# Dealing one store's rows unevenly over the 16 DMA engines: dV of head 15 in a decode-attention gradient kernel

## The chip, the cores and the metric

The kernel runs on one core of a Trainium2 chip. The metric is the device time of one execution, in microseconds (us). Each figure below is the median of several executions, with lowest and highest in brackets. The kernel before took 402.59 us (402.49 to 402.77, 3 runs) when it was handed over. Every run quoted here counts as a fast one (none lies over 1.5% above the fastest of its kernel). The profile of a run spans about 2 us less than its device time (400.6 against 402.6).

## The reference, cut to what matters

```python
def _A_ref(x, k_cache, v_cache, wq, wo):        # one query token, H=32 heads, Sk=4096, Dh=128, D=640, bf16
    q = (x @ wq).reshape(B, Sq, H, Dh).transpose(0, 2, 1, 3)
    p = softmax(einsum("bhqd,bhkd->bhqk", q, k_cache) * Dh ** -0.5)
    o = einsum("bhqk,bhkd->bhqd", p, v_cache)
    return o.transpose(0, 2, 1, 3).reshape(B, Sq, H * Dh) @ wo
# _B_ref: a dense layer 640 -> 1728 -> 640 with mish;  g = sigmoid((x * gate_w).sum(-1))
return g * a + (1 - g) * b
# reference(): this output, and its gradients by x, k_cache, v_cache, wq, wo, w1, b1, w2, gate_w
```

K and V have 32 x 4096 x 128 elements of 2 bytes, 33.6 MB each, and their gradients dK and dV are as large. So of the 164.93 MB that the kernel moves, 134 MB are these four, and some 31 MB are the weights and their gradients. One head is 1 MB (1024 KB) of K, of V, of dK and of dV.

## The kernel before

Loads of K, V and the weights are issued by the sync engine (SP), on one hardware queue. Nearly all gradients are stored by the gpsimd engine (POOL), on the software queue. Both queues run on the same 16 DMA engines. A tile of one head has 128 rows (partitions) of 8192 B. A plain DMA of it puts 8 rows on each of the 16 engines.

```python
KB, VB = 4, 4
outs = ctx.enter_context(tc.tile_pool(name="outs", bufs=5))        # dK and dV tiles on their way out

def load_k(h):                                                      # load_v is alike
    if h < H:
        kts[h] = kv_in.tile([P, J, Dh], BF16, name="Kn", tag="Kn", bufs=KB)
        nc.sync.dma_start(kts[h][:], Kv[h])

def load_wo(g):                                                     # g: a group of G = 4 heads
    if g < NG:
        wos[g] = wts.tile([P, G, D], BF16, name="wo_g", tag="wo_g", bufs=3)
        nc.sync.dma_start(wos[g][:], wo_v[g])
...
def dwo():                                 # the gradient overwrites the weight tile and is stored from it
    for i in range(G):
        nc.vector.tensor_scalar(wos[g][:, i, :], da_bc[:], fs["o4"][:, i:i + 1], None, ALU.mult)
    (nc.sync if g == NG - 1 else nc.gpsimd).dma_start(dwo_v[g], wos[g][:])
...
for h in range(H):
    hh, g = h % G, h // G
    if hh == 3:
        load_wo(g + 2)                     # waits for the dwo store that still reads this buffer ...
        if g % 2 == 0:
            load_wq(g // 2 + 1)
    load_k(h + 3)                          # ... and these stand behind it in the same queue
    load_v(h + 3)
    ...
    period(h)
...
dwq_l = wts.tile([P, RC, GD], BF16, name="dwq_l", tag="wo_g", bufs=3)
...
nc.sync.dma_start(dwq_v[:, :, CL:], dwq_l[:])                       # the last store of the kernel
```

A new `wo_g` tile can be loaded only when the store of an older `dwo` out of the same buffer has landed on all the engines. And the K and V loads of the next head are issued after that load by the same sequencer.

The kernel before already deals a few dV stores unevenly (heads 5, 12, 19 and 26). It cuts the rows into several DMAs; for heads 5 and 26 it first resets the cursor, the place from which the software queue starts dealing rows to engines:

```python
if half == 1:
    if h % 7 == 5 and h < H - 3:
        spread(h // 7, dVv[h], st["dV"])
    else:
        ring(h).dma_start(dVv[h], st["dV"][:])

def spread(i, dst, t):
    ...
    if i % 3 == 0:
        nc.gpsimd.inc_swdge_sem([], [], mode="reset_dge_cursor")
    for a, b in (((120, 125), (0, 120), (125, 128)), ((0, 14), (14, 119), (119, 128)), ((0, 8), (8, 128)))[i % 3]:
        nc.gpsimd.dma_start(out[a:b, :], src[a:b, :], max_dma_last_dim=J * Dh)
```

## Time and profile before

| | |
|---|---|
| device time | 402.59 us |
| bytes moved | 164.93 MB, 412 GB/s on average |
| DMA share of the stretches between 12 and 385 us | 1.01 to 1.02 |
| busiest compute engines | DVE 303.5 us, PE 296.6 us |
| last computation ends, last store issued, last store landed | 387.3, 391.9, 399.5 us |

These are lines of the page of the kernel before: busy time of each engine, the span in 40 slices of 10.0 us (digits are busy tenths), and the queues with packets, MB and share. `q1` is the queue of the loads, `q0` the software queue of the stores, `q8` fetches instructions.

```profile
span 400.6 us, 13611 instructions
PE 296.6 (74%) x5872; PEld 268.1 (67%) x5872; DVE 303.5 (76%) x791; ACT 177.1 (44%) x411; POOL 47.2 (12%) x94
DMA  8999999999999999999999999999999999999995
GB/s 288 420 415 397 421 426 417 418 423 422 425 419 424 421 422 419 419 424 422 427 415 426 422 423 419 418 428 422 421 424 423 422 421 417 423 422 416 425 378 232
DMA packets 28360, 164.93 MB, mean 412 GB/s; under 512 B 3260, under 2 KB 3964, under 8 KB 12556
q1 hardware_dynamic: 17136, 93.41, 56.5%
q0 software_dynamic: 11104, 70.64, 42.3%
q8 instruction: 46, 0.75, 0.7%
```

The DMA engines are full from start to end, and DVE and PE have a quarter of the span free.

No view names DMA engines. In the packet records, however, a packet starts 3 or 4 ns before its predecessor on the same engine ends, so the packets can be sorted into 16 streams. For the kernel before that gives:

- The 46 instruction fetches (16 KB, 0.99 us each) go round robin to eight of the 16 engines, six each to six of them ("heavy") and five each to two. I call these eight the fetching engines.
- Seven engines without fetches ("light") end by 396 us.
- One more without fetches, at position 4 counted from the reset cursor, has some 15 us of stretched packets (packets that take longer than usual for their size). The existing spreads give it less. It ends at 399.1 us.

### The profile page before, as it was taken

What the parts mean: (1) busy time and instruction counts of PE and PEld (TensorE: products, weight loads), DVE (VectorE), ACT (ScalarE), POOL (GpSimd) and SP (SyncE); (2) the same over time, 40 slices, a digit from 0 to 9 for tenths busy, and PEclk for the clock granted to TensorE, in tenths of its full rate; (3) what the DMA queues carried; (4) which work ended last, traced back from release to release, by engine and by line L of the source; (5) the groups of instructions that cost most, each with busy time, mean ns of one, the idle gap of its engine ahead of it and who ended that gap; (6) DMA issues with size and microseconds to landing.
All of it is one profiled execution on the core that took longest, in us unless ns stands there. A gap on an engine that the chain in (4) does not pass through costs nothing.

```text
span 400.6 us, 13611 instructions
## 1 busy us (share of the span) xinstructions
PE 296.6 (74%) x5872; PEld 268.1 (67%) x5872; DVE 303.5 (76%) x791; ACT 177.1 (44%) x411; POOL 47.2 (12%) x94
## 2 busy tenths in 40 slices
PE   0688898778888788778885988819887888888200
PEld 0588787668777678668875878718776777777200
DVE  2438766646799999856688799837999997899850
ACT  1355555324554455325543555605545455545000
POOL 0001101021110111211110113101110121111000
PEclk9999999959999999959998899977999999999655
DMA  8999999999999999999999999999999999999995
GB/s 288 420 415 397 421 426 417 418 423 422 425 419 424 421 422 419 419 424 422 427 415 426 422 423 419 418 428 422 421 424 423 422 421 417 423 422 416 425 378 232
DMA packets 28360, 164.93 MB, mean 412 GB/s; under 512 B 3260, under 2 KB 3964, under 8 KB 12556
## 3 DMA queue, kind: packets, MB, share of 16 engines
q1 hardware_dynamic: 17136, 93.41, 56.5%
q0 software_dynamic: 11104, 70.64, 42.3%
q8 instruction: 46, 0.75, 0.7%
q14 instruction: 14, 0.11, 0.1%
q10 hardware_dynamic: 60, 0.01, 0.0%
HBM read 82.03 MB, written 82.03 MB: 410 GB/s over the span
## 4 chain that ended last, share of the span: by engine, by line
DVE 36%; DMA 34%; PE 17%; issue 5%; ACT 4%; SPq 0%; POOL 0%; ACTq 0%; POOLq 0%
DMA Kn<-in_A_k_cache_dram 29%; DVE dK_sb L612 9%; DVE dV_sb L612 8%; PE tr L587 7%; DVE junk L385 4%; DMA out_dram<-wo_g 4%; ACT tT L589 4%; PE sA L667 3%; DVE junk L288 3%; PE sA L596 2%; PE sB L720 2%; DVE junk L537 2%; DMA vec_rows<-in_gate_w_dram 1%; DVE wo_g L374 1%; DVE dj L707 1%
## 5 line engine op out<-in xcount | busy, mean ns | idle before, releaser
L589 ACT COPY tT<-tr 128x512 f32<-128x512 f32 x256 | 142.3, 588 | 133.9 <-PE tr L587 133.1
L596 PEld LDWEIGHTS <-tT 128*128 128x128 bf16 x2048 | 79.8, 98 | 40.1 <-ACT tT L589 34.6
L587 PE MATMUL tr<-ident_f,Kn 128*128 128x128 f32 x512 | 82.0, 298 | 9.7 <-DMA Kn<-in_A_k_cache_dram 9.7
L612 DVE TENSOR_TENSOR dV_sb<-p_bf,qd 128x2048 bf16<-128x2048 bf16 x64 | 78.0, 1218 | 0.2 <-issue 0.2
L612 DVE TENSOR_TENSOR dK_sb<-ds_bf,qd 128x2048 bf16<-128x2048 bf16 x64 | 77.7, 1216 | 0.0
L587 PE MATMUL tr<-ident_f,Vn 128*128 128x128 f32 x512 | 72.5, 277 | 0.0
L587 PEld LDWEIGHTS tr<-ident_f,Kn 128*128 128x128 f32 x512 | 61.2, 152 | 11.2 <-issue 11.2
L596 PE MATMUL sA<-qd,tT 128*128 128x48 bf16 x1024 | 48.8, 187 | 23.7 <-ACT dq_all L725 12.7
L587 PEld LDWEIGHTS tr<-ident_f,Vn 128*128 128x128 f32 x512 | 55.9, 141 | 0.0
L596 PE MATMUL sB<-qd,tT 128*128 128x48 bf16 x1024 | 46.1, 183 | 0.0
L667 PEld LDWEIGHTS <-Vn 128*128 128x128 bf16 x1024 | 30.2, 95 | 10.4 <-issue 10.4
L667 PE MATMUL sA<-e_bf,Vn 128*128 128x48 bf16 x1024 | 30.7, 183 | 7.7 <-DVE zs L687 6.1
L629 POOL DMA_DIRECT2D out_dram<-dK_sb x30 | 17.3, 576 | 138.6 <-DVE rz L689 90.6
L720 PE MATMUL sB<-ds_bf,Kn 128*128 128x48 bf16 x1024 | 32.1, 185 | 1.4 <-DVE ds_bf L709 1.4
L671 DVE TENSOR_REDUCE m<-sA 128x1 f32<-128x32 f32 x32 | 6.1, 189 | 35.2 <-PE sA L596 28.5
L720 PEld LDWEIGHTS <-Kn 128*128 128x128 bf16 x1024 | 29.4, 97 | 1.6 <-issue 1.6
L642 POOL DMA_DIRECT2D out_dram<-dV_sb x26 | 14.1, 544 | 136.8 <-DVE o_all L712 50.0
L288 DVE SCALAR_TENSOR_TENSOR junk<-wo_g,da_bc 128x640 bf16<-128x640 bf16 x32 | 26.3, 821 | 2.6 <-ACT da_bc L229 1.1
L385 DVE SCALAR_TENSOR_TENSOR junk<-wq_g,dq_bc 128x1024 bf16<-128x1024 bf16 (+1 forms) x25 | 25.1, 1005 | 0.2
L707 DVE TENSOR_SCALAR_CACHE_REDUCE dj<-sB,rz 128x128 f32<-128x128 f32 x32 | 11.1, 346 | 9.2 <-PE sB L701 9.2
L691 ACT ACTIVATE p_bf<-e_bf,rz 128x64 bf16<-128x64 bf16 x32 | 11.1, 348 | 13.6 <-DVE rz L689 10.7
L698 DVE SCALAR_TENSOR_TENSOR pj<-sB,e_bf 128x32 f32<-128x32 f32 x32 | 6.1, 190 | 12.5 <-PE sB L596 12.4
(152 smaller groups left out, 275.5 us busy)
## 6 DMA issues: line engine op xcount, KB each, us to landing
Kn<-in_A_k_cache_dram SPq DMA_DIRECT2D x32, 1024.0 KB, 23.1
Vn<-in_A_v_cache_dram SPq DMA_DIRECT2D x32, 1024.0 KB, 27.5
out_dram<-dK_sb POOLq DMA_DIRECT2D x30, 1024.0 KB, 11.7
out_dram<-dV_sb POOLq DMA_DIRECT2D x26, 1024.0 KB, 11.8
wq_g<-in_A_wq_dram SPq DMA_DIRECT2D x4, 1280.0 KB, 23.7
wo_g<-in_A_wo_dram SPq DMA_DIRECT2D x8, 640.0 KB, 16.7
out_dram<-wo_g POOLq DMA_DIRECT2D x7, 640.0 KB, 12.2
out_dram<-dwq_t SPq DMA_DIRECT2D x4, 896.0 KB, 18.3
```

The costliest lines, as they stand in the source:

```text
L288: nc.vector.scalar_tensor_tensor(junk[:, 0:D], in0=wos[g][:, i, :], scalar=1.0, in1=da_bc[:], op0=ALU.mult, op1=ALU.mult, accum_out=gp["do ...
L385: nc.vector.scalar_tensor_tensor(junk[:, c0:c1], in0=wqs[w][:, rc, c0:c1], scalar=1.0, in1=dq_bc[:, w * WG * Dh + c0:w * WG * Dh + c1], op ...
L587: nc.tensor.transpose(tp[:, t, :], flat[:, k * P:(k + 1) * P], ident_f[:])
L589: nc.scalar.copy(sb[:].rearrange("p a b -> p (a b)"), tp[:].rearrange("p a b -> p (a b)"))
L596: nc.tensor.matmul(out[:, 2 * k:2 * k + W], lhsT=tb[:, t, par, :], rhs=vec[:, par, :].unsqueeze(1).to_broadcast([P, W // 2, 2]), start=(pa ...
L612: nc.vector.tensor_tensor(dst[:, a:b, :].rearrange("p j (a b) -> p j a b", b=2), col[:, a:b, :].unsqueeze(2).to_broadcast([P, n, Dh // 2, 2]),
L629: ring(h).dma_start(dKv[h], st["dK"][:])
L642: ring(h).dma_start(dVv[h], st["dV"][:])
L667: nc.tensor.matmul(O, lhsT=vts[h][:, j, :], rhs=st["e"][:, j:j + 1].to_broadcast([P, W]), start=(j == 0), stop=(j == J - 1))
L691: nc.scalar.activation(p_bf[:], e[:].unsqueeze(2).to_broadcast([P, J, 2]), ACT.Copy, scale=rz[:])
L707: nc.vector.tensor_scalar(dj[:], PT, rz[:], None, ALU.mult, ALU.add, accum_out=dd[:])
L720: nc.tensor.matmul(DQ, lhsT=kts[h][:, j, :], rhs=ds[:, j, 0:1].to_broadcast([P, W]), start=(j == 0), stop=(j == J - 1))
```

## The change

The intent is to even the load of the engines: head 15's dV gets 17 rows on each of the seven engines at positions 8 to 14 and one row on each of positions 0 to 7. The last row is cut into 16 pieces of 512 B, one for each engine. Heads 12 and 19 get the same cut as heads 5 and 26, and the cursor is reset at each of these stores.

```diff
         if half == 1:
-            if h % 7 == 5 and h < H - 3:
-                spread(h // 7, dVv[h], st["dV"])
+            if h in SPREAD:
+                spread(SPREAD[h], dVv[h], st["dV"])
             else:
                 ring(h).dma_start(dVv[h], st["dV"][:])
 
-    def spread(i, dst, t):
+    S15 = ((120, 125), (0, 120), (125, 128))
+    SPREAD = {5: S15, 12: S15, 15: ((0, 8), (8, 127), (127, 128)), 19: S15, 26: S15}
+
+    def spread(parts, dst, t):
 ...
-        if i % 3 == 0:
-            nc.gpsimd.inc_swdge_sem([], [], mode="reset_dge_cursor")
-        for a, b in (((120, 125), (0, 120), (125, 128)), ((0, 14), (14, 119), (119, 128)), ((0, 8), (8, 128)))[i % 3]:
+        nc.gpsimd.inc_swdge_sem([], [], mode="reset_dge_cursor")
+        for a, b in parts:
             nc.gpsimd.dma_start(out[a:b, :], src[a:b, :], max_dma_last_dim=J * Dh)
```

## The prediction

> **What bounds the kernel.** The page gives 164.93 MB in 400.6 us, 412 GB/s; the stretch table a DMA share of 1.01 or 1.02 in every stretch from 12 to 385 us, against 303.5 us busy on DVE and 296.6 on PE. In the timeline the last computation (the copy of fin_rows) ends at 387.3 us; 13 us of pure stores follow. So DMA bounds it, and its most loaded engines end it: dwq_l is computed by 381.2 us but issued at 391.9, when an earlier store on its semaphore has landed on all engines, and lands at 399.5.
>
> **Which engines are most loaded.** No view names DMA engines. But in the packet records a packet starts 3 or 4 ns before its predecessor on the same engine ends, so I separated the packets into 16 streams, each with the sizes that its queues require. (Positions below count from the reset cursor.)
> - The 46 instruction packets (16 KB, 0.99 us each) go round robin to eight engines, about 5.5 us each; the others get none.
> - These eight end together, at 398 to 399 us, without idle time. Seven have no fetches, run up to 16 us ahead in the loads and end by 396. One more (position 4) has no fetches, but 14 us of stretched packets; the existing spreads avoid it.
> - The Trainium skill ("DMA: Bandwidth & Descriptors", "Why a DMA increments its semaphore by 16 and not by 1") says that SWDGE uses k consecutive engines from a round-robin cursor. The trace agrees: of head 5, the 5 rows land on positions 0 to 4, the 120 on all but 4, the 3 on 4 to 6. From heads 5, 12 and 19: positions 0 to 3 are light, 4 slow, 5 and 6 fetch, 7 to 12 hold four fetching and two light, 13 to 15 two fetching and one light.
>
> **What the change does.** Positions 8 to 14 get 17 rows of head 15 instead of 8, the others one. (The last row is split into 16 pieces of 512 B.) Making heads 12 and 19 alike takes one row from positions 7 to 15. By the sets above, 8 to 14 hold at least three of the four fetching engines in 7 to 12 and one in 13 to 15: at least four of the eight that end the kernel. Four light engines (0 to 3) are relieved, who need it least.
>
> **Cost.** A row as two 4096 B packets takes 2 x 156 ns, as one of 8192 B 306 ns. A heavy fetching engine gains 17 x 0.311 - 8 x 0.306 - 0.31 = +2.5 us. It never idles and both its queues must drain, so nearly all of it reaches the end: later loads, and the landing that releases dwq_l, come up to 2.5 us later. Relieving the rest helps nothing, as the slowest engine decides. Compute instructions are unchanged; the extra POOL issues are hidden.
>
> **Prediction.** 402.6 + 2.5 = about 405.0 us, 402.7 to 406.4. Faster by over 2%: 0.01; within 2%: 0.97; slower by over 2%: 0.02.
>
> **What would show it.** dV of head 15 lands some 10 us later than before (now 12 to 17 us after issue); dwq_l issued near 394 instead of 391.9, landing near 402; bytes and DVE and PE busy time unchanged.
>
> **What would make it wrong.** If positions 8 to 14 were just the seven light engines, the slowest would lose 7 rows and the time fall by 1 to 2 us, to about 401. If the 119 rows were dealt as 8 rows to each of 15 engines, nothing would change.

## More of the kernel before

The sync queue's waits of the kernel before (engine, line, what it waited for, then us in total, times, and the longest in us). L121 is `load_k`, L136 is `load_wo`.

```profile
SPq L121 <- PE sB L720: 168.3, 20, 17.8
SPq L136 <- DMA out_dram<-wo_g: 58.0, 5, 13.3
```

The second line is the wait for the dwo store. It takes 58.0 us in five waits, and during each of them no load is issued. In the timeline of the sync engine (start, duration, line, what) it looks like this around 230 us:

```profile
224.72 0.33 SPq L121 DMA_DIRECT2D Kn<-in_A_k_cache_dram  x1
225.10 0.50 SPq L126 DMA_DIRECT2D Vn<-in_A_v_cache_dram  x1
238.00 0.33 SPq L136 DMA_DIRECT2D wo_g<-in_A_wo_dram  x1
238.42 0.43 SPq L131 DMA_DIRECT2D wq_g<-in_A_wq_dram  x1
238.94 0.69 SPq L121 DMA_DIRECT2D Kn<-in_A_k_cache_dram  x1
```

And the chain of waits of the kernel before passes through it:

```profile
223.24 14.71 DMA out_dram<-wo_g
...
238.94 31.03 DMA Kn<-in_A_k_cache_dram
```

From one load to the next there are 12.9 us, and the two slices from 220 to 240 us still have 422 and 423 GB/s, as the queue of loads already issued lasts that long.

## The result, and the profile after

The changed kernel took 407.40 us (407.14 to 407.88, 4 runs) against 402.68 us (402.49 to 403.44, 4 runs) of the kernel before on the same chip. The ratio is 1.0115, with an interval of 1.0098 to 1.0133. A ratio here is the mean time of one kernel's fast runs over that of the other's of the same rounds, so it is not quite the ratio of the medians quoted. The change costs 4.7 us, or 1.2%. That is inside the band of 2% in which kernels count as the same, and 1.0 us above the top of the predicted range.

The page of the kernel after (40 slices of 10.1 us):

```profile
span 405.5 us, 13618 instructions
PE 295.8 (73%) x5872; PEld 267.6 (66%) x5872; DVE 303.5 (75%) x791; ACT 177.1 (44%) x411; POOL 49.2 (12%) x97
DMA  7999999999999999999999999999999999999984
GB/s 293 420 416 401 421 422 420 420 420 424 420 423 423 422 422 416 422 424 422 422 418 422 424 415 350 380 423 421 422 422 422 424 422 421 420 422 419 423 345 181
DMA packets 28936, 164.93 MB, mean 407 GB/s; under 512 B 3694, under 2 KB 4414, under 8 KB 13260
```

The bytes and the work of DVE and PE are unchanged. The row of GB/s shows something that nobody had predicted: in the 25th and 26th slice (243 to 264 us) the rate falls to 350 and 380 GB/s, where it was 419 and 418. The digits of the DMA row stay at 9 there: the engines are busy but slow. The missing rate is (419 - 350 + 418 - 380) GB/s over 10.14 us, or 1.08 MB, and at 420 GB/s that is worth 2.6 us.

The changed store is issued at 197 us, and the dip comes 45 us later. What lies between is in the waits and the timeline of the sync queue after the change:

```profile
SPq L121 <- PE sB L722: 158.4, 20, 16.6
SPq L136 <- DMA out_dram<-wo_g: 70.5, 5, 23.0
```

```profile
221.61 0.33 SPq L121 DMA_DIRECT2D Kn<-in_A_k_cache_dram  x1
221.99 0.64 SPq L126 DMA_DIRECT2D Vn<-in_A_v_cache_dram  x1
245.68 0.33 SPq L136 DMA_DIRECT2D wo_g<-in_A_wo_dram  x1
246.10 3.73 SPq L131 DMA_DIRECT2D wq_g<-in_A_wq_dram  x1
249.92 2.41 SPq L121 DMA_DIRECT2D Kn<-in_A_k_cache_dram  x1
```

No load was issued for 23.7 us (221.99 to 245.68), where it had been 12.9 us (225.10 to 238.00). The `dwo` store of group 4 was issued at nearly the same time, but it landed late. From the semaphore's 16 increments, one per engine (my own reading of the trace):

```
                                  issued   first engine landed   last engine landed
dV of head 15, before             197.33   209.50                214.37
dV of head 15 (119 rows), after   197.01   214.14                222.31
dwo of group 4, before            223.24   233.10                237.95
dwo of group 4, after             223.65   235.19                245.62
```

The Trainium skill ("DMA: Bandwidth & Descriptors", "Why a DMA increments its semaphore by 16 and not by 1") says that only the full 16 means that all data has landed, and that all 16 engines post their increment on the software queue whatever the shape. The trace agrees: `load_wo` is issued at 245.68 us, 0.06 us after the sixteenth increment, although the first engine had done its part 10 us earlier.

The lines of the stores in the issues of each kernel (KB each, median us from issue to landing). Before:

```profile
out_dram<-dV_sb POOLq DMA_DIRECT2D x26, 1024.0 KB, 11.8
out_dram<-wo_g POOLq DMA_DIRECT2D x7, 640.0 KB, 12.2
```

After. The third line is the DMA of 119 rows:

```profile
out_dram<-dV_sb POOLq DMA_DIRECT2D x25, 1024.0 KB, 13.0
out_dram<-wo_g POOLq DMA_DIRECT2D x7, 640.0 KB, 13.2
out_dram<-dV_sb POOLq DMA_DIRECT2D x1, 952.0 KB, 25.3
```

The table by stage (length, busy us and instructions of PE, PEld, DVE, ACT and POOL, granted clock, DMA share, GB/s), of the stretch in which the sync queue waits and of the one after it. Before:

```profile
238.00:246.00 8.00, 6.39 (x145) 5.74 (x144) 7.59 (x21) 3.43 (x9) 1.87 (x3) 1.00 1.01 422
246.00:256.00 10.00, 8.71 (x183) 7.84 (x181) 8.20 (x21) 7.27 (x15) 2.78 (x5) 1.00 1.02 418
```

After:

```profile
238.00:246.00 8.00, 6.89 (x133) 6.33 (x130) 7.66 (x20) 4.29 (x10) 1.92 (x3) 1.00 0.99 392
246.00:256.00 10.00, 8.76 (x180) 7.89 (x177) 8.22 (x24) 6.80 (x14) 2.27 (x4) 1.00 1.00 358
```

Compute hardly differs, so it did not cause the dip. The DMA engines read as busy (1.00) at 358 GB/s. The streams tell more: the leading engines have no load left from 233 us on, and from 246 to 249 us fewer than one of the 16, on average, is moving one. Among the packets of the software queue, which then run alone on most engines, those of 4096 B are stretched: of 158 between 243 and 252 us, 67 took over 190 ns, many of them 300 to 600, where 159 is usual. Those of 8192 B took 8% longer than usual on average. The packets of 4096 B belong to the store of head 19, which is cut in the same way as that of head 5:

```profile
241.68 1.92 POOL L652 DMA_DIRECT2D out_dram<-dV_sb  x3 [3.88 <-DVE dV_sb L612]
```

Summed over 16 engines, packets between 240 and 260 us took 39.1 us longer than their usual time, where it had been 3.8, and the engines stood idle for 5.4 us more. That is (35.3 + 5.4) / 16 = 2.5 us per engine, close to the 2.6 from the rate.

The end of the kernel, in its timeline (the last computation on ACT, and the last store on the sync queue). Before:

```profile
387.06 0.26 ACT L829 COPY fin_rows<-fin_ps 15x128 bf16<-15x128 bf16 x1 [12.76 <-PE fin_ps L827]
...
391.90 0.38 SPq L793 DMA_DIRECT2D out_dram<-dwq_l  x1
```

After:

```profile
388.73 0.25 ACT L831 COPY fin_rows<-fin_ps 15x128 bf16<-15x128 bf16 x1 [12.77 <-PE fin_ps L829]
...
396.60 0.38 SPq L795 DMA_DIRECT2D out_dram<-dwq_l  x1
```

The last computation is 1.7 us later, the last store 4.7 us. Its landing moves from 399.46 to 404.41 us.

The streams also confirm the dealing. The 8 rows of the first DMA lie on positions 0 to 7. The 119 rows lie as 34 packets of 4096 B (17 rows) on each of positions 8 to 14. Among these seven are six fetching engines, all those with six fetches, and one light one. The heavy engines moved 10.426 MB each, where they had moved 10.360. That is 65.5 KB, or 8 rows, more. They end at 400.6 to 404.1 us, and all other engines at 399.4 to 399.5.

### The profile page after: what moved, and what is told of

Same layout as the page of the kernel before. It is cut to its first block, busy times and chain, and to the rows that moved or that the text cites. A ratio compares the mean times of both kernels' runs of the same rounds, so it can differ in the third digit from the quotient of the medians.

```text
span 405.5 us, 13618 instructions
## 1 busy us (share of the span) xinstructions
PE 295.8 (73%) x5872; PEld 267.6 (66%) x5872; DVE 303.5 (75%) x791; ACT 177.1 (44%) x411; POOL 49.2 (12%) x97
## 4 chain that ended last, share of the span: by engine, by line
DVE 40%; DMA 32%; PE 17%; ACT 4%; issue 2%; ACTq 0%; DVEq 0%
DMA Kn<-in_A_k_cache_dram 26%; DVE dK_sb L612 9%; DVE dV_sb L612 9%; PE tr L587 7%; DMA out_dram<-dK_sb 5%; DVE junk L385 4%; DVE junk L288 3%; ACT tT L589 3%; PE sA L669 2%; PE sA L596 2%; PE sB L722 2%; DVE junk L537 1%; DVE junk L494 1%; DVE wo_g L374 1%; DMA vec_rows<-in_gate_w_dram 1%
## 5 line engine op out<-in xcount | busy, mean ns | idle before, releaser
L596 PE MATMUL sA<-qd,tT 128*128 128x48 bf16 x1024 | 48.6, 187 | 23.6 <-ACT dq_all L727 12.7
L288 DVE SCALAR_TENSOR_TENSOR junk<-wo_g,da_bc 128x640 bf16<-128x640 bf16 x32 | 26.3, 821 | 1.7 <-ACT da_bc L229 1.1
L709 DVE TENSOR_SCALAR_CACHE_REDUCE dj<-sB,rz 128x128 f32<-128x128 f32 x32 | 11.1, 346 | 13.3 <-PE sB L703 13.3
L278 PE MATMUL qc_ps<-cols_bf,wq_g 128*128 128x1 bf16 x160 | 5.2, 164 | 14.4 <-DMA wq_g<-in_A_wq_dram 14.4
```

Of the source, the lines that this page charges most:

```text
L288: nc.vector.scalar_tensor_tensor(junk[:, 0:D], in0=wos[g][:, i, :], scalar=1.0, in1=da_bc[:], op0=ALU.mult, op1=ALU.mult, accum_out=gp["do ...
L596: nc.tensor.matmul(out[:, 2 * k:2 * k + W], lhsT=tb[:, t, par, :], rhs=vec[:, par, :].unsqueeze(1).to_broadcast([P, W // 2, 2]), start=(pa ...
L709: nc.vector.tensor_scalar(dj[:], PT, rz[:], None, ALU.mult, ALU.add, accum_out=dd[:])
```

## The experiments

My theory after reading the result had two parts: (a) the fetching engines end last and got more rows; (b) the laggards make the dwo store land late, and the sync queue's wait for it holds up the loads until the engines run dry. The rivals were the realigning of heads 12 and 19, the splitting into half-size packets as such, and (a) alone.

### 1. Without head 15's entry

```diff
-    SPREAD = {5: S15, 12: S15, 15: ((0, 8), (8, 127), (127, 128)), 19: S15, 26: S15}
+    SPREAD = {5: S15, 12: S15, 19: S15, 26: S15}
```

> The changed kernel without its head 15 part: only heads 12 and 19 are dealt like 5 and 26. Theory (17 rows on fetching engines do it all): 402.6 us, within 0.5 of the kernel before. Rival (the new dealing of heads 12 and 19, with up to 2 more rows on two fetching engines, has a share): 403.3 us or more.

It took 402.94 us (402.49 to 403.09), against 402.69 of the kernel before in the same rounds. The ratio is 1.0002 (0.9987 to 1.0017). The realigning of heads 12 and 19 and the extra cursor resets cost nothing; the whole loss comes from head 15.

### 2. Head 15 in three pieces, 8 rows on each engine

```diff
-    15: ((0, 8), (8, 127), (127, 128))
+    15: ((0, 64), (64, 112), (112, 128))
```

> Head 15 still stored by a cursor reset and three DMAs in packets of 4096 B, but 64, 48 and 16 rows, so that every engine gets 8 rows. Theory (the uneven dealing is the cost): as e1_no_h15 within 0.5 us. Rival (three issues, descriptor making and half-size packets are the cost): over 2 us more than e1_no_h15.

The runs were 402.93, 403.15, 404.51 and 408.16 us: median 403.83, ratio 1.0047 (0.9991 to 1.0104). The profiled run took 402.93. Three of the four runs say that splitting costs between nothing and 2 us, and one outlier keeps the interval wide. It is far from the 4.7 us, but the exact cost of the splitting is not settled.

### 3 and 4. K and V loads ahead of the wo load

If the sync queue issues the K and V loads first, the wait for the dwo store cannot hold them up in that step. The edit goes on the kernel after (3) and on the kernel before (4), as a control:

```diff
+        load_k(h + 3)
+        load_v(h + 3)
         if hh == 3:
             load_wo(g + 2)
             ...
-        load_k(h + 3)
-        load_v(h + 3)
```

> The changed kernel, but at every fourth head the loads of K and V are issued ahead of the load of wo, so the sync queue no longer holds them back while it waits for the store of dwo. Theory (2.5 us of added rows, plus some 2 us because loads were held up behind that wait): about 2 us below the changed kernel, 405.0 to 405.7, and 2.5 us above e4_before_kv_first. Rival (all of the 4.8 us is added work on the loaded engines): 407 us, unchanged.

> The kernel before with the same reordering of loads, as the base of e3_after_kv_first. Theory: there the wait for the dwo store (13.3 us at most) starves no engine, so 402.6 us within 0.5. Rival (the wait already costs in the kernel before): 401.5 us or less.

The changed kernel with the edit took 408.8 us (408.14 to 409.86), ratio 1.0152; the kernel before with it took 404.2 us (403.25 to 404.68), ratio 1.0027. The difference is 4.6 us, as large as without the edit. My expectation missed. The reason is in the waits and the page of experiment 3: the wait was shortened but it had only moved to the loads of the next head. The longest is still 12.7 us, and the dips stay.

```profile
SPq L136 <- DMA out_dram<-wo_g: 18.9, 5, 12.7
```

The reorder also costs 1.5 us by itself; why was not looked into. So this pair neither supports nor refutes part (b): it did not take the hold-up away.

### 5. The rows on light engines instead

Positions 0 to 3 are light. Here they get 20 rows each, and all others 4.

```diff
-    15: ((0, 8), (8, 127), (127, 128))
+    15: ((0, 68), (68, 116), (116, 128))
```

> Head 15 dealt more unevenly than in the changed kernel, but onto four engines without instruction fetches: positions 0 to 3 get 20 rows, all others 4. Theory (what counts is which engines get the rows): the fetching engines lose 4 rows, 1.2 us, and of the light ones the latest gains 3.7 us with 2.7 us in hand, so 401.5 to 403.7 us. Rival (a head stored unevenly costs as such, by holding later stores back): 405.5 us or more.

The runs were 402.72, 402.83, 404.96 and 405.74 us: median 403.9, ratio 1.0026 (0.9970 to 1.0081). That is about 3.5 us below the changed kernel, although the rows are dealt with a like unevenness (20 to 4 against 17 to 1). That speaks for part (a), that it counts which engines get the rows. But half of the runs lie above the range that I expected, the longest wait for a dwo store is 26.3 us, and one slice falls to 356 GB/s: light engines with many rows hold up the dwo store as well. Two of the seven runs of the kernel before in the same rounds were also at 404.76 and 405.22 us, so the two higher runs need not come from the edit. The mean can't be split between the two parts, so for their sizes this run is inconclusive.

The profile of this run (402.83 us) shows one thing more. The waits, and the table by stage for 2 us in which no engine moved a load:

```profile
SPq L136 <- DMA out_dram<-wo_g: 87.3, 5, 26.3
```

```profile
241.00:243.00 2.00, 1.80 (x26) 1.80 (x27) 1.96 (x6) 1.41 (x6) 0.00 (x0) 1.00 1.02 427
```

For 5.3 us (240.6 to 245.9) no packet of a load starts on any engine, and the store packets, all of 8192 and 5120 B, take their usual time (1.01 of it). Where all 16 engines have stores they move 427 GB/s; the dip of this run lies from 243 us on, where engines stand idle and then the first packets of the new loads are slow. Head 19's store of 4096 B packets was issued only at 249.3 us, when loads ran again, and is not stretched (160 ns on average). So the lack of loads alone does not slow the stores. In the changed kernel it met a store in 4096 B packets.

### 6. The same rows in three portions

Heads 10, 15 and 21 each give positions 8 to 14 three rows more than usual (11 instead of 8), again 9 in all for each of them, as in the change.

```diff
+    MV = ((0, 8), (8, 57), (57, 121), (121, 128))
-    SPREAD = {5: S15, 12: S15, 15: ((0, 8), (8, 127), (127, 128)), 19: S15, 26: S15}
+    SPREAD = {5: S15, 12: S15, 19: S15, 26: S15, 10: MV, 15: MV, 21: MV}
```

> The same 9 extra rows on positions 8 to 14, but 3 in each of heads 10, 15 and 21 (11 rows instead of 8), so no store holds later ones back for long. Theory (of the 4.8 us, 2.5 are rows and the rest a hold-up of loads in the middle): 2.5 to 3 us above e1_no_h15, 405.2 to 406.0, with the sync queue's longest wait for the dwo store under 17 us (23.0 in the changed kernel). Rival (all 4.8 us is added work on the loaded engines): 407.4.

It took 406.74 us (406.50 to 407.31), ratio 1.0084 (1.0047 to 1.0121). I had expected the small portions to leave the loads alone; they did not. The page and the waits of this run:

```profile
GB/s 289 423 417 402 421 426 417 419 418 426 423 421 422 423 391 389 423 420 423 423 420 420 425 424 391 399 420 421 423 403 419 424 423 421 423 418 422 422 366 170
```

```profile
SPq L121 <- PE sB L723: 134.8, 17, 16.8
SPq L136 <- DMA out_dram<-wo_g: 85.0, 5, 25.7
```

There are now three shallower dips (391 and 389, 391 and 399, 403) in place of one deep one, and the longest wait is 25.7 us. After head 10 alone, with a lag of three rows per engine, the wait that ends at 196.8 us already took 18.6 us, against 11.9 in the kernel before and 14.2 in experiment 1. The next one took the 25.7. That the lag stays because the fetching engines have no idle time to catch up in fits this, but was not tested. The first dip is of another kind: the wait before it took 12.2 us, no longer than before (13.3). It lies where head 10's own store, now in 4096 B packets (184 ns each on average), meets a moment of few loads.

### 7 and 8. A fourth wo_g buffer

This takes the wait's cause away: with four buffers a load of `wo_g` goes into a buffer whose dwo store was issued a group (four heads) earlier. Room for it comes from one buffer less of another pool. The edit goes on the kernel after (7) and the kernel before (8).

```diff
-    tsb = ctx.enter_context(tc.tile_pool(name="tsb", bufs=4))
+    tsb = ctx.enter_context(tc.tile_pool(name="tsb", bufs=3))
...
-    wos[g] = wts.tile([P, G, D], BF16, name="wo_g", tag="wo_g", bufs=3)
+    wos[g] = wts.tile([P, G, D], BF16, name="wo_g", tag="wo_g", bufs=4)
...
-    dwq_l = wts.tile([P, RC, GD], BF16, name="dwq_l", tag="wo_g", bufs=3)
+    dwq_l = wts.tile([P, RC, GD], BF16, name="dwq_l", tag="wo_g", bufs=4)
```

> The changed kernel with a fourth wo buffer (one buffer less for the transposed tiles makes room), so the load of wo needs no fresh dwo store. Reordering in e3 only put the wait one head later. Theory (the hold-up of loads behind that wait is some 2 us): 2.5 us (to 3.2) above e8_before_wo4. Second theory (loads stop anyway, because light engines run ahead only as far as four K and V buffers allow): still 4 us or more above e8.

> The kernel before with the same four wo buffers and three for the transposed tiles: the base of e7. Expected 402.6 us within 1 either way, as DMA bounds it; if it is much slower, the missing buffer matters and e7 is read against it with care.

The changed kernel with four buffers took 404.23 us (404.15 to 404.38), ratio 1.0020 (0.9984 to 1.0056). The kernel before with four took 402.67 us (402.41 to 402.71), ratio 0.9980 (0.9944 to 1.0016). The edit does nothing for the kernel before, and takes 3.2 us (407.40 - 404.23) off the changed one. These lines are from the page, the waits and the table by stage of experiment 7:

```profile
GB/s 287 419 415 403 421 423 417 421 421 422 426 418 424 423 421 416 418 424 424 424 416 420 423 422 418 419 423 425 420 424 425 424 421 422 422 412 397 418 365 215
```

```profile
SPq L121 <- PE sB L722: 214.5, 26, 16.6
```

```profile
238.00:246.00 8.00, 6.81 (x152) 6.16 (x148) 7.61 (x21) 3.92 (x10) 2.45 (x4) 1.00 1.02 422
246.00:256.00 10.00, 8.72 (x183) 7.85 (x182) 8.21 (x21) 7.26 (x15) 2.27 (x4) 1.00 1.01 415
```

The wait of L136 for a dwo store is gone, and with it the dip: 418 and 419 GB/s where the changed kernel had 350 and 380. The extra packet time between 240 and 260 us is back at 4.9 us. The dwo store itself was not faster: it was issued at 221.87 and landed at 247.67 us, even later than without the fourth buffer, but nobody waited for it. This is the test that settles part (b): the hold-up of the loads is needed for the dip. It does not say how large the dip would be without head 19's cut store in the same place; no run changed that alone.

What is left between 7 and 8 is 404.23 - 402.67 = 1.6 us. The last store lands at 401.29 against 399.76 us, which is 1.5. That is part (a), the rows on the heavy engines, and it is smaller than the 2.5 to 3.2 that I had expected. The streams say why: the six heavy engines end at 398.1 to 398.6 us in 8 and at 400.6 to 401.0 in 7, which is 2.6 us later on average. But in 8 position 4 ends last, at 399.4, so only 1.5 us of it (401.0 - 399.4) reaches the end. So of the 4.7 us the rows account for about 1.6, and the hold-up of the loads for about 3.1, of which the dip explains 2.5 or 2.6.

### 9. Three portions and a fourth buffer

The edits of experiments 6 and 7 together.

```diff
+    SPREAD = {5: S15, 12: S15, 19: S15, 26: S15, 10: MV, 15: MV, 21: MV}
+    ... tsb bufs=3, wo_g bufs=4
```

> e6 (9 extra rows on positions 8 to 14 over three heads) with the four wo buffers of e7 and e8. Theory (the excess of e6 over the added rows is again the sync queue held up by the dwo store, up to 25.7 us there): 404.2 to 405.4, near e7, with no wait for a dwo store. Rival (the excess comes from the uneven dealing itself): 406.5 or more.

It took 404.96 us (404.57 to 405.32), ratio 1.0051 (1.0021 to 1.0080). It came as expected: 1.8 us below experiment 6 and 2.3 us above experiment 8. The same rows, moved without the hold-up, again cost about 2 us.

### 10 to 12. Looking for a better version

With the wait out of the way, the opposite dealing should gain: rows from fetching engines to light ones. In 10 it is the cut of experiment 5 in head 15. In 11 it is a milder cut in three heads. In 12 it is that milder cut in two heads, and two more heads get the cut that spares position 4.

```diff
+    15: ((0, 68), (68, 116), (116, 128))                                   # 10
+    LT = ((0, 15), (15, 40), (40, 120), (120, 128))
+    SPREAD = {..., 8: LT, 15: LT, 22: LT}                                  # 11
+    SPREAD = {..., 9: S15, 23: S15, 15: LT, 21: LT}                        # 12
+    ... tsb bufs=3, wo_g bufs=4                                            # all three
```

> e5 (20 rows of head 15 on positions 0 to 3, which fetch no instructions, 4 on all others) with four wo buffers. Theory: fetching engines lose 4 rows, 1.2 us, and no hold-up: 1 to 1.5 us below e8 (402.67), so 401.2 to 401.8. Rival (an uneven store costs as such even here): 402.7 or more.

> Four wo buffers, and in heads 8, 15 and 22 the light positions 15 and 0 to 3 get 10 or 11 rows, the others 6 or 7. Fetching engines lose 3 to 6 rows, 0.9 us at least; the light ones gain up to 9 rows, 2.8 us, which they have in hand. Theory: 401.5 to 402. Rival: no gain over e8, 402.6 or more.

> In e10 and e11 the fetching engines ended about 1 us earlier than in e8 and the time stayed, as the packet streams show since the engine at position 4 (20 us of stretched packets) or one of positions 0 to 3 ended last, at 399 us. So here four wo buffers, the dealing that avoids position 4 in two more heads (9 and 23), and the mild dealing of e11 in heads 15 and 21 only: position 4 loses 14 rows, fetching engines 0 to 4, positions 0 to 3 gain 8. Theory (the last engine decides, and now three kinds of engines come closer together): 401.5 to 402.2, at best 0.25% under the kernel before. Rival (another limit, as the end of the computation): 402.6 or more.

| | median us | lowest to highest | ratio (interval) |
|---|---|---|---|
| 10 | 402.75 | 402.47 to 403.25 | 0.9996 (0.9970 to 1.0023) |
| 11 | 402.71 | 402.48 to 403.46 | 0.9997 (0.9973 to 1.0021) |
| 12 | 402.46 | 401.75 to 402.79 | 0.9987 (0.9965 to 1.0009) |

All three equal the kernel before, so the expected gain of 1 us and more did not come. The streams show where it went in 10. The heavy engines now end at 397.0 to 397.4 us (398.1 to 398.6 in experiment 8), but one of the light engines at positions 0 to 3 ends at 399.6 and position 4 at 398.8. In 11, position 4 ends last, at 399.4. The heavy engines were not the last in experiment 8 (position 4 was, at 399.4), so taking rows from them alone could not move the end, and the light engines, which ended by 395.5, had some 4 us to spare: 12 rows more take that up. No version was found that clearly beats the kernel before.

## Why the prediction was wrong

The direction was right, and the mechanism it named is there, but it makes the smaller part of the loss (1.6 of 4.7 us). A second path, which it did not have, makes the larger part. 405.0 was predicted, with 402.7 to 406.4 as range, and 407.4 was measured.

- **"So DMA bounds it, and its most loaded engines end it."** Right that DMA bounds it. In the kernel before, the last engine is position 4, at 399.1 us, and not a fetching one (398.7 at the latest). After the change the heavy engines end last, and the last store's landing moves with them (399.46 to 404.41 us).
- **"8 to 14 hold at least ... four of the eight that end the kernel."** Right, and an understatement: six of the seven are fetching engines.
- **"A heavy fetching engine gains ... +2.5 us ... nearly all of it reaches the end."** The gain of one engine was right: 2.6 us on average (7 against 8). That nearly all of it reaches the end was wrong. With the hold-up taken away the rows cost 1.6 us, as position 4 ended 0.8 us after the last of the heavy engines and 1.2 after their average. When the rows are dealt in three heads they cost 2.3 us (9 against 8); why more was not shown.
- **"Later loads, and the landing that releases dwq_l, come up to 2.5 us later."** This is the step that failed, and it made the miss: the later landing was counted as one more effect of the same 2.5 us, and not as a wait that stops the loads. The sum had only one term, the work of the slowest engine. A store that lags does not merely end later; it holds its buffer, and here a load waited for that buffer with all other loads behind it. The wo load came 7.7 us later (238.00 to 245.68 us), the loads ran dry, and the engines ran at 350 and 380 GB/s for 20 us. This term, missing from the prediction, measured about 3.1 us (4.7 - 1.6); the fourth buffer took off 3.2. It could have been looked for: the profile before showed a wait of 58.0 us for dwo stores, and the chain of waits passed through one of them.
- **What would show it.** The dV of head 15 landed 8 us later (222.3 instead of 214.4; "some 10 us" was said), and bytes and busy times stayed. dwq_l was issued at 396.6 us and landed at 404.4, not "near 394" and "near 402": later by 2.6 and 2.4 us, most of the missing term.
- **What would make it wrong.** Neither case came true: positions 8 to 14 are not the light engines, and the 119 rows were not dealt over 15 engines.

Two things stay open. It is not known why the store packets of 4096 B were stretched so much when few engines had loads. In the kernel before, packets of the same queue that were alone on an engine were not stretched (1.000 of their usual time, against 1.20 after), but nearly all of those were of 8192 B, and after the change it is the ones of 4096 B that are stretched (1.7, against 1.05 for 8192 B). No run varies the size of the packets alone. And the split of 1.6 and 3.1 us takes the two costs to be additive, which no run tests.

## What to carry to other kernels

In this kernel, where DMA is the limit, a lag put on some engines was still there at the end (2.6 us on the heavy ones), and a store completed with its slowest engine (dwo of group 4: first 235.19, last 245.62 us). So when you judge a change in how a store is dealt, look at which engine really ends last, and by how much, and also at who waits for the stores behind it. The waits of the issuing queue, before the change, show where to look. A buffer more at that wait took the sensitivity away here (3.2 us), though it gained nothing by itself.

## What the Trainium skill lacked or had wrong

- "Runtime: NRT & Kernel Launch", section "Instruction fetch mechanics", says that instructions come in blocks of 16 KiB by the sequencer's own DMA queue, and that the cost of crossing from one block to the next is "mostly hidden". The trace agrees with the block size (46 packets of 16 KB). What the fetches cost this kernel no run shows. They take 0.99 us each of an engine's time and went to only eight of the 16 engines, five or six to each; the six engines with six fetches end at 398.1 to 398.7 us, the seven light ones by 396. No page says which engines carry them.
- "DMA: Bandwidth & Descriptors", section "Why a DMA increments its semaphore by 16 and not by 1": that the software queue uses k consecutive engines from a cursor was confirmed by the dealing of 119 rows as 7 times 17. The section doesn't say what the other engines get: in the streams each of them has as many packets of 4 B (34) as the used ones have of data.
- The same page, section "Queues, rings and completion order": that an engine goes round robin between its queues packet by packet agrees with the streams (in the kernel before, four of five packets follow one of the other queue). The consequence is missing, that engines with a deeper queue of stores make later stores of that queue land late (dwo of group 4, issued 26.6 us after the changed store, at 245.62 instead of 237.95 us).
- The same page, section "Where 436 GB/s comes from", says that for transfers between HBM and SBUF the HBM side, about 358 GB/s, is the limit. This one core moved 412 GB/s on average and 415 to 428 in most slices, reading and writing together. The limit did not hold here; the number is nearer to the 435 of the fabric there, and to a measurement of 425 that the same passage calls near fabric-rate.
- The same page, section "Latency and other measured facts", says that engines 7 and 15 are usually slower. In these runs one engine of 16 was (some 15 to 21 us of stretched packets); its number isn't to be seen in the trace.
- No page has it that packets of 4096 B of the software queue, when hardly any engine had a load left, took 276 ns on average instead of 159 (243 to 252 us of the changed kernel), so that busy engines moved only 350 to 380 GB/s. Packets of 8192 and 5120 B with no load on any engine were not slowed (427 GB/s in experiment 5). The cause is open.
